# Row-packed 64-row products fed by full transposes, pairs first, and a second layer one group behind

## The chip, the cores and the metric

The kernel runs on one core of a Trainium2 chip. The metric is device time in microseconds: the median of three timed runs, and beside it one profiled execution with its trace.

## The reference

An mLSTM cell runs over four batches of eight heads (768 steps, 40 values a head). Its output, 3072 rows of 320 values, goes through a mixture of eight experts, of which each row uses the one with the largest logit.

```python
# cell, for each step t: C, n are decayed and added to, then read with q
h_tilde = np.einsum('bhde,bhe->bhd', C, qt)
denom = np.maximum(np.abs(nq), 1.0)
y[:, :, t] = o * h_tilde / denom
# experts; x has 3072 rows of D = 320, w1 is (8, 320, 1024), w2 is (8, 1024, 320)
logits = x @ w_gate
expert_idx = np.argmax(logits, axis=1)
...
for e in range(E):
    h = np.maximum(x_sorted[lo:hi] @ w1[e], 0.0)
    y_sorted[lo:hi] = h @ w2[e]
return gate_w[:, None] * y_sorted[inv_perm]
```

## The kernel before

The cell is done in 24 blocks of 128 steps. Rows are then scattered to DRAM by expert and read back in tiles of 128 rows. An expert gets three tiles in any case: a group of two, which is read early, and a group of one. Five more tiles are for what overflows, and for those the weights of the expert concerned are copied within SBUF (`wx`). Two groups of two (experts 0 and 1) run while the cell ends; the other six groups of two, eight groups of one and the five overflow tiles run in the main loop below.

The 320 values of a row are 128 + 128 + 64. The 64 last are done as pairs: w1's last 64 rows are held twice, on partitions 0 to 63 for the first half of the hidden columns and on 64 to 127 for the second half, so that two 64-row matmuls can run side by side. For that the last 64 columns of a tile are transposed onto both partition halves.

```python
    def weights_in(e, n=1):                                   # w1, cast to bf16 on the way
        nc.gpsimd.dma_start(
            w1_all[:, e, : FL * F].rearrange("p (a f) -> p a f", f=F),
            moe_w1[e, : FL * 128, :].rearrange("(a p) f -> p a f", p=128),
        )
        for i in range(2):
            nc.gpsimd.dma_start(
                w1_all[64 * i : 64 * i + 64, e, FL * F :], moe_w1[e, FL * 128 :, i * HF * 128 : (i + 1) * HF * 128],
            )

    def weights_out(e0, n):                                   # w2
        e = slice(e0, e0 + n)
        nc.gpsimd.dma_start(
            w2_all[:, e].rearrange("p e a d -> p (e a) d"), moe_w2[e].rearrange("e (a p) d -> p (e a) d", p=128),
        )
...
    def turn(g):
        n = g["n"]
        src = g["xg"] if "xg" in g else xg[g["e"]][g["k"]]
        g["xT"] = spot("xT", [128, DB, n * 128], BF16)
        tp = spot("tp", [128, DB, n * 128], BF16)
        for j in range(n):
            for db in range(DB):
                at = src[:, j, db * 128 : min(Dm, (db + 1) * 128)]
                if db < FL:
                    nc.tensor.transpose(tp[:, db, j * 128 : (j + 1) * 128], at, ident_b[:])
                    continue
                for r in range(2):
                    nc.tensor.transpose(tp[64 * r : 64 * r + 64, db, j * 128 : (j + 1) * 128], at, ident_b[:])
        nc.vector.tensor_copy(g["xT"], tp)

    def layer1(g, u):
        n = g["n"]
        per = 4 // n
        w, xT = g["w"][0], g["xT"]
        v = u // 2 * per
        if u == 0:
            g["h"] = spot("h", [128, FB, n * 128], BF16)
        if u % 2 == 0:
            g["hp"] = [spot("hp", [128, per, n * 128], F32) for _ in range(2)]
            for i in range(per):
                for a in range(2):
                    c = FL * F + (v + i) * 128
                    r = slice(64 * a, 64 * a + 64)
                    nc.tensor.matmul(
                        g["hp"][a][:, i, :], lhsT=w[r, c : c + 128], rhs=xT[r, FL, :], start=(i == 0), stop=False,
                        skip_group_check=True,
                    )
        a = u % 2
        hp = g["hp"][a]
        for i in range(per):
            for db in range(FL):
                c = db * F + (a * HF + v + i) * 128
                nc.tensor.matmul(
                    hp[:, i, :], lhsT=w[:, c : c + 128], rhs=xT[:, db, :], start=False, stop=(db == FL - 1),
                    skip_group_check=True,
                )
        dst = g["h"][:, a * HF + v : a * HF + v + per, :]
        if a == 0:
            nc.vector.tensor_relu(dst, hp)
        else:
            nc.scalar.activation(dst, hp, AF.Relu)

    def layer2(g, j):
        zp = spot(g.get("zp", "zp"), [128, Dm], F32)
        for fb in range(FB):
            nc.tensor.matmul(
                zp, lhsT=g["h"][:, fb, j * 128 : (j + 1) * 128], rhs=g["w"][1][:, fb, :],
                start=(fb == 0), stop=(fb == FB - 1),
            )
        zo = spot("zo", [128, Dm], F32)
        nc.scalar.copy(zo, zp)
        at = g["to"] if "to" in g else s_idx[:, g["e"], g["si"] + j : g["si"] + j + 1]
        ins = nc.gpsimd.indirect_dma_start(
            out=out[:, :], out_offset=bass.IndirectOffsetOnAxis(ap=at, axis=0),
            in_=zo, in_offset=None, bounds_check=N - 1, oob_is_err=False,
        )
        if g.get("apart", True):
            apart(ins, "rows_out")
        if j + 1 < g["n"]:
            pause()

    def pause():
        nc.gpsimd.memset(rest[:], 0.0)

```

`zp` of the two early groups is taken from the same four PSUM buffers as `hp`. The main loop has four `hp`, two `zp` and two `tp` buffers, three each of `h` and `xT`, and sixteen of `zo`. In it the order is fixed as written:

```python
    order = [(2, 0), (3, 0), (0, 1), (1, 1), (4, 0), (2, 1), (5, 0), (3, 1), (4, 1), (6, 0), (5, 1), (7, 0), (6, 1), (7, 1)]
    groups = [...] + [dict(n=1, x=x) for x in range(XU)]      # (expert, part): part 0 has two tiles, part 1 has one
    ...
    pieces = extras()
    ready(groups[0])
    for i, g in enumerate(groups):
        nw = g.get("e", E) + 3
        x = i - len(order) + XW
        if 0 <= x < XU:
            groups[len(order) + x]["w"] = fetch(expert_of(x))
        if g.get("k") == 0 and nw < E:
            weights_in(nw, 1)
            weights_out(nw, 1)
        for u in range(FB * g["n"] // 4):
            layer1(g, u)
        if i + 1 < len(groups):
            ready(groups[i + 1])
        if 1 <= i < 5:
            next(pieces, None)
        if i == 5:
            for e_ in range(E):
                blank(e_)
            for x in range(XU):
                collect(groups[len(order) + x], row_of(x), invx[:, x : x + 1])
        for j in range(g["n"]):
            layer2(g, j)
```

`ready` computes the target rows and does `turn`, the transposes. `fetch` copies an overflow tile's weights. `warm(n)` issues n matmuls of 512 columns whose result isn't used; `warm(3)` stands at the last block of the cell and `warm(2)` after the first early transposes.

Of the kernel before, what the change touches and what calls it, by code (L numbers as in the profile page):

```python
# [8 lines left out]
F32 = mybir.dt.float32  # L9
BF16 = mybir.dt.bfloat16  # L10
# [9 lines left out]
def kernel(  # L20
# [13 lines left out]
    nc = tc.nc  # L34
    B, H, S, D = q.shape
    BH = B * H
    NB = S // 128
    N = B * S
    Dm = H * D
    E = moe_w_gate.shape[1]  # L40
    F = moe_w1.shape[2]
    FB = F // 128
    NT = N // 128
    PR = H // 2
    DP = 64
# [5 lines left out]
    dch = []  # L51
    d0 = 0
# [5 lines left out]
    FL = DB - 1  # L58
    HF = FB // 2
    wch = [d0 if dsz == 128 else Dm - 128 for d0, dsz in dch]  # L60
    assert NT * 128 == N and FB * 128 == F and D <= DP and dch[FL][1] == 64


    NJ = 3
# [110 lines left out]
    xg = [(x_all[:, NE * e : NE * (e + 1), :], x_all[:, NE * E + e : NE * E + e + 1, :]) for e in range(E)]  # L175

    def weights_in(e, n=1):
        nc.gpsimd.dma_start(
            w1_all[:, e, : FL * F].rearrange("p (a f) -> p a f", f=F),
            moe_w1[e, : FL * 128, :].rearrange("(a p) f -> p a f", p=128),  # L180
        )
        for i in range(2):
            nc.gpsimd.dma_start(
                w1_all[64 * i : 64 * i + 64, e, FL * F :], moe_w1[e, FL * 128 :, i * HF * 128 : (i + 1) * HF * 128],
            )

    def weights_out(e0, n):
        e = slice(e0, e0 + n)
        nc.gpsimd.dma_start(
            w2_all[:, e].rearrange("p e a d -> p (e a) d"), moe_w2[e].rearrange("e (a p) d -> p (e a) d", p=128),  # L190
        )

    def apart(ins, group):
# [24 lines left out]
    def spot(kind, shape, dtype):  # L218
        i = turns[kind] = turns.get(kind, -1) + 1
        at = spots[kind][i % len(spots[kind])]  # L220
        if isinstance(at, tuple):
            tag, pool = at
            return pool.tile(shape, dtype, name=kind, tag=tag)[:]
        n = 1
        for m in shape[1:]:
            n *= m
        at = at[:, :n]
        return at.rearrange("p (a b) -> p a b", b=shape[2]) if len(shape) == 3 else at

    def turn(g):  # L230
        n = g["n"]
        src = g["xg"] if "xg" in g else xg[g["e"]][g["k"]]
        g["xT"] = spot("xT", [128, DB, n * 128], BF16)
        tp = spot("tp", [128, DB, n * 128], BF16)
        for j in range(n):
            for db in range(DB):
                at = src[:, j, db * 128 : min(Dm, (db + 1) * 128)]
                if db < FL:
                    nc.tensor.transpose(tp[:, db, j * 128 : (j + 1) * 128], at, ident_b[:])
                    continue  # L240
                for r in range(2):
                    nc.tensor.transpose(tp[64 * r : 64 * r + 64, db, j * 128 : (j + 1) * 128], at, ident_b[:])
        nc.vector.tensor_copy(g["xT"], tp)

    def layer1(g, u):
        n = g["n"]
        per = 4 // n
        w, xT = g["w"][0], g["xT"]
        v = u // 2 * per
        if u == 0:  # L250
            g["h"] = spot("h", [128, FB, n * 128], BF16)
        if u % 2 == 0:
            g["hp"] = [spot("hp", [128, per, n * 128], F32) for _ in range(2)]
            for i in range(per):
                for a in range(2):
                    c = FL * F + (v + i) * 128
                    r = slice(64 * a, 64 * a + 64)
                    nc.tensor.matmul(
                        g["hp"][a][:, i, :], lhsT=w[r, c : c + 128], rhs=xT[r, FL, :], start=(i == 0), stop=False,
                        skip_group_check=True,  # L260
                    )
        a = u % 2
        hp = g["hp"][a]
        for i in range(per):
            for db in range(FL):
                c = db * F + (a * HF + v + i) * 128
                nc.tensor.matmul(  # L267
                    hp[:, i, :], lhsT=w[:, c : c + 128], rhs=xT[:, db, :], start=False, stop=(db == FL - 1),
                    skip_group_check=True,
                )  # L270
        dst = g["h"][:, a * HF + v : a * HF + v + per, :]
# [23 lines that stand above are left out]
# [12 lines left out]
    with tc.tile_pool(name="ring", bufs=1) as ring_pool, \  # L307
# [256 lines left out]
        def warm(n):  # L564
            j = ps1.tile([128, 512], F32, name="junk", tag="tk")
            for _ in range(n):
                nc.tensor.matmul(
                    j[:], lhsT=ident_b[:], rhs=st[NT - 1]["dA"][:].rearrange("p j t -> p (j t)"), start=True, stop=True,
                )
# [37 lines left out]
        for s in range(-3, NT):  # L607
            P, odd = (s - 4) // 2, s % 2
            last = s == NT - 1
            do(scores, s + 1)  # L610
            do(transposes, s + 2)
            if s == -3:
                masks()
            if s == -2:
                gates()
                router()
            do(values, s + 2)
            if odd and s > E and sent <= (s - 5 if s > 2 * PE_ + 4 else s - 6):
                send(sent)
                sent += 1  # L620
            if s == NT - 5:
                weights_in(0, 1)
            pair = not odd and 0 <= P
            if pair:
                gate(P)
            do(states, s)
            do(load, s + 6 if s >= -1 else -1)
            if pair:
                rank(P, s - 1)
            if last:  # L630
                warm(3)
            do(xtrans, s - 1)
            do(ogate, s + 2)
            do(attend, s)
            if pair:
                place(P)
                if P == PE_:
                    even_out(s - 1)
            if s == 2 * PE_ + 4:
                keep_rows(s - 4)  # L640
                keep_rows(s - 3)
            elif s != 2 * PE_ + 5:
                do(keep_rows, s - 4)
            do(rows, s)
            if odd and 0 <= (s - 3) // 2:
                logits((s - 3) // 2, s - 1)
                choose((s - 3) // 2)
                count((s - 3) // 2)
            upto = s - 4 if s >= 2 * PE_ + 4 else s - 5
            if s > E and sent <= upto:  # L650
                send(sent)
                sent += 1
            if 0 <= s < E:
                clear(s)
            late_consts(s + 1)
            if s == 2 * PE_ + 5:
                for e in range(E):
                    receive(e, 0)
            if s == NT - 4:
                weights_out(0, 1)  # L660
            if s == NT - 3:
                weights_in(1, 1)
            if s == NT - 2:
                weights_out(1, 1)
# [12 lines left out]
        first, second = early  # L677
        targets(0, 0)
        turn(first)
        warm(2)  # L680
        xtrans(NT - 1)
        layer1(first, 0)
        logits(P0 + 1, NT)
# [131 lines left out]
# [16 lines that stand above are left out]
                blank(e_)  # L831
            for x in range(XU):
                collect(groups[len(order) + x], row_of(x), invx[:, x : x + 1])
        for j in range(g["n"]):
            layer2(g, j)
    one_order.close()
    nx = nc.values_load(xe[0:1, NX : NX + 1], min_val=0, max_val=NX)
    with tc.If(nx > XU):
# [40 lines left out]
```

## Time and profile before

| | before |
|---|---|
| time, median of three runs | 217.75 us (216.98 to 218.1) |
| span of the profiled run | 217.2 us |
| mean granted TensorE clock | 0.984 |
| TensorE matmul busy | 192.3 us (89%) in 2048 matmuls |
| TensorE weight loads busy | 151.8 us (70%) |
| VectorE, ScalarE, GpSimd busy | 57%, 54%, 64% |
| moved by DMA | 44.32 MB, mean 204 GB/s |
| chain that ended last | TensorE 46%, GpSimd 20%, "issue" 14%, VectorE 9%, DMA 5% |

PE is TensorE's matmuls, PEld its weight loads, DVE VectorE, ACT ScalarE, POOL GpSimd, SP the queue of the sync engine. Matmuls overlap in the array, so the time from one start to the next counts, not the length of one. A line such as L267 is a line of the kernel printed above; an arrow (out<-in) names what is written and read; "[0.44 <-DMA x]" says that the engine sat idle for 0.44 us until x. The chain that ended last is followed back from the last instruction, at each step to what released it. "issue" is idle time that nothing in the profile explains.

### The profile page before, as it was taken

What the parts mean: (1) busy time and instruction counts of PE and PEld (TensorE: products, weight loads), DVE (VectorE), ACT (ScalarE), POOL (GpSimd) and SP (SyncE); (2) the same over time, 40 slices, a digit from 0 to 9 for tenths busy, and PEclk for the clock granted to TensorE, in tenths of its full rate; (3) what the DMA queues carried; (4) which work ended last, traced back from release to release, by engine and by line L of the source; (5) the groups of instructions that cost most, each with busy time, mean ns of one, the idle gap of its engine ahead of it and who ended that gap; (6) DMA issues with size and microseconds to landing.
All of it is one profiled execution on the core that took longest, in us unless ns stands there. A gap on an engine that the chain in (4) does not pass through costs nothing.

```text
span 217.2 us, 5727 instructions
## 1 busy us (share of the span) xinstructions
PE 192.3 (89%) x2048; PEld 151.8 (70%) x2057; DVE 124.8 (57%) x410; ACT 117.3 (54%) x273; POOL 139.3 (64%) x238
## 2 busy tenths in 40 slices
PE   1299999999999999979899998969999986999970
PEld 1168788899998899978786755647667654676740
DVE  7746667677787878797776342345833332333320
ACT  2458657797789897896751552323333322332330
POOL 6036786644869889749999489838656786253221
PEclk9999999999999999999998899999999999999996
DMA  7999999989999989994799999999999999985310
GB/s 139 197 198 190 205 205 204 231 156 254 178 193 173 195 161 206 193 204 84 142 184 262 222 205 150 193 254 233 216 229 245 231 290 408 409 317 201 149 46 10
DMA packets 120782, 44.32 MB, mean 204 GB/s; under 512 B 102506, under 2 KB 115821, under 8 KB 120752
## 3 DMA queue, kind: packets, MB, share of 16 engines
q1 hardware_dynamic: 105456, 25.34, 55.9%
q0 software_dynamic: 14832, 18.38, 40.3%
q8 instruction: 17, 0.28, 0.5%
q10 hardware_dynamic: 464, 0.21, 0.4%
q14 instruction: 13, 0.11, 0.2%
HBM read 39.30 MB, written 9.37 MB: 224 GB/s over the span
## 4 chain that ended last, share of the span: by engine, by line
PE 46%; POOL 20%; issue 14%; DVE 9%; DMA 5%; ACT 3%; POOLq 1%; ACTq 0%; DVEq 0%
POOL out_dram L287 7%; PE hp L474 6%; PE zp L280 5%; DMA w_all<-in_moe_w_dram 5%; PE hp L406 5%; PE tk L368 4%; POOL x_sorted L579 4%; PE dC L414 4%; PE hp L267 4%; PE tq L368 3%; PE xt L451 3%; PE sA L386 3%; PE sA L381 2%; POOL x_sb L444 2%; POOL rest L297 2%
## 5 line engine op out<-in xcount | busy, mean ns | idle before, releaser
L273 DVE TENSOR_SCALAR h<-hp 128x512 bf16<-128x512 f32 x25 | 17.3, 692 | 40.6 <-PE hp L267 26.3
L287 POOL DMA_INDIRECT out_dram<-zo,s_idx x20 | 20.0, 1002 | 16.3 <-ACT zo L285 10.0
L275 ACT ACTIVATE h<-hp 128x512 bf16<-128x512 f32 x25 | 14.9, 597 | 25.2 <-PE hp L267 19.9
L579 POOL DMA_INDIRECT x_sorted<-x_all,slots x24 | 25.3, 1054 | 4.9 <-issue 3.9
L444 POOL TENSOR_TENSOR x_sb<-x_sb,den 128x320 f32<-128x320 f32 x23 | 16.8, 729 | 17.2 <-DVE den L442 17.1
L280 PE MATMUL zp<-w_all,h 128*128 128x320 bf16 x160 | 24.5, 300 | 3.5 <-DMA w_all<-in_moe_w_dram 1.6
L280 PEld LDWEIGHTS <-h 128*128 128x128 bf16 x200 | 17.7, 98 | 13.2 <-DVE h L273 2.7
L285 ACT COPY zo<-zp 128x320 f32<-128x320 f32 x25 | 10.7, 426 | 27.2 <-PE zp L280 23.7
L267 PEld LDWEIGHTS <-w_all 128*128 128x128 bf16 x256 | 18.4, 98 | 5.6 <-issue 3.4
L393 ACT CAST dB<-sB 128x512 bf16<-128x512 f32 x24 | 14.0, 585 | 13.7 <-PE sB L387 11.5
L267 PE MATMUL hp<-xT,w_all 128*128 128x128 bf16 (+1 forms) x224 | 21.1, 243 | 0.0
L406 PE MATMUL hp<-C_sb,qT 104*128 104x82 f32 x160 | 20.7, 272 | 0.0
L368 PE MATMUL tk<-ident,kq 128*104 128x128 f32 x96 | 16.4, 296 | 4.2 <-DMA kq<-in_k_dram 4.2
L406 PEld LDWEIGHTS hp<-C_sb,qT 104*128 104x128 f32 x160 | 19.4, 192 | 0.3
L453 ACT COPY xT<-xt 128x384 f32<-128x384 f32 x24 | 11.6, 482 | 13.5 <-PE xt L451 12.5
L356 POOL CAST vAb<-vA 128x328 bf16<-128x328 f32 x24 | 11.0, 459 | 11.7 <-DVE vA L354 11.7
L474 PE MATMUL hp<-wg_sb,xT 128*128 128x8 f32 x144 | 18.0, 258 | 0.0
L414 PE MATMUL dC<-vA,kq 128*104 128x82 f32 x160 | 17.9, 254 | 0.0
L394 POOL TENSOR_SCALAR_AFFINE_SELECT dB<-dB 128x512 bf16<-128x512 bf16 x24 | 16.5, 689 | 1.7 <-ACT dB L393 1.5
L474 PEld LDWEIGHTS hp<-wg_sb,xT 128*128 128x128 f32 x144 | 17.4, 195 | 0.1
L391 DVE TENSOR_TENSOR dA<-sA,cmask 128x512 bf16<-128x512 f32 x24 | 16.0, 669 | 1.4 <-PE sB L387 1.4
L414 PEld LDWEIGHTS dC<-vA,kq 128*104 128x104 f32 x160 | 16.3, 172 | 0.0
(160 smaller groups left out, 455.8 us busy)
## 6 DMA issues: line engine op xcount, KB each, us to landing
wx<-w_all SPq DMA_DIRECT2D x10, 640.0 KB
w_all<-in_moe_w_dram POOLq DMA_DIRECT2D x8, 640.0 KB
w_all<-in_moe_w_dram POOLq DMA_DIRECT2D x8, 512.0 KB
kq<-in_k_dram SPq DMA_DIRECT2D x24, 160.0 KB
kq<-in_q_dram SPq DMA_DIRECT2D x24, 160.0 KB
v<-in_v_dram SPq DMA_DIRECT2D x24, 160.0 KB
o_sb<-in_o_gate_dram SPq DMA_DIRECT2D x24, 160.0 KB
x_sorted<-zrow POOLq DMA_DIRECT2D x8, 241.5 KB
```

Of the source, the lines that this page charges most:

```text
L267: nc.tensor.matmul(hp[:, i, :], lhsT=w[:, c : c + 128], rhs=xT[:, db, :], start=False, stop=(db == FL - 1), skip_group_check=True,)
L273: nc.vector.tensor_relu(dst, hp)
L280: nc.tensor.matmul(zp, lhsT=g["h"][:, fb, j * 128 : (j + 1) * 128], rhs=g["w"][1][:, fb, :], start=(fb == 0), stop=(fb == FB - 1),)
L287: ins = nc.gpsimd.indirect_dma_start(out=out[:, :], out_offset=bass.IndirectOffsetOnAxis(ap=at, axis=0), in_=zo, in_offset=None, bounds_ch ...
L368: nc.tensor.transpose(tp[:, j, :], two(d[n], j), ident[:])
L391: nc.vector.tensor_tensor(d["dA"][:], sA[:], cmask[:, None, :].to_broadcast([128, PR, 128]), op=ALU.mult)
L394: nc.gpsimd.affine_select(d["dB"][:], d["dB"][:], compare_op=ALU.is_ge, fill=0.0, base=0, pattern=[[0, PR], [1, 128]], channel_multiplier=-1,)
L406: nc.tensor.matmul(hp[:, 2 * j * D1 : (2 * j + 2) * D1], lhsT=d["qT"][:, j, :], rhs=st["C"][:, j].rearrange("p h d -> p (h d)"), start=(j ...
L414: nc.tensor.matmul(st["dC"][:, j], lhsT=two(d["k"], j), rhs=d["vA"][:, 2 * j : 2 * j + 2, :], start=(c == 0 and j == 0), stop=True, skip_g ...
L444: eng.tensor_tensor(x3d, x3d, den[:].unsqueeze(2).to_broadcast([128, H, D]), op=ALU.mult)
L474: nc.tensor.matmul(lg[:, i * E : (i + 1) * E], lhsT=st[t]["xT"][:, db * 128 : (db + 1) * 128], rhs=wg_sb[:, db, :], start=(fresh and i == ...
L579: ins = nc.gpsimd.indirect_dma_start(out=xs[:, :], out_offset=bass.IndirectOffsetOnAxis(ap=slots[:, t : t + 1], axis=0), in_=x_all[:, t, : ...
```

## The change

Four things are altered in the expert stage. First, each tile is transposed four times in full, from columns 0, 192, 128 and 64 on, 128 columns each; the third has the columns 128 to 191 on partitions 0 to 63 and the fourth has them on 64 to 127, so these two feed the 64-row pairs, and the first two the full matmuls. The pairs thus use w1's rows 128 to 191. The aim is that transposes and the matmuls around them use the array in the same way. Second, all pairs of a group are issued first, into all product buffers of the group, where a two-tile group did half of them before each half of its full matmuls. Third, in the main loop a group's second layer is issued after the next group's first layer, so that its relu need not be waited for. Fourth, w2 is loaded so that a partition gets two neighbouring rows in one run of 2560 bytes instead of two runs of 1280; hidden unit 256a + 2p + j then sits on partition p, and w1's columns are read with a step of two to match. Besides, `warm` has two more matmuls in one place and one more in the other.

```diff
--- before.py
+++ after.py
@@ -58,7 +58,9 @@
     FL = DB - 1
     HF = FB // 2
     wch = [d0 if dsz == 128 else Dm - 128 for d0, dsz in dch]
-    assert NT * 128 == N and FB * 128 == F and D <= DP and dch[FL][1] == 64
+    assert NT * 128 == N and FB * 128 == F and D <= DP and Dm == 5 * 64
+    parts = [0, 192, 128, 64]
+    NP = len(parts)
 
 
     NJ = 3
@@ -175,19 +177,22 @@
     xg = [(x_all[:, NE * e : NE * (e + 1), :], x_all[:, NE * E + e : NE * E + e + 1, :]) for e in range(E)]
 
     def weights_in(e, n=1):
+        at = moe_w1.offset + e * Dm * F
         nc.gpsimd.dma_start(
             w1_all[:, e, : FL * F].rearrange("p (a f) -> p a f", f=F),
-            moe_w1[e, : FL * 128, :].rearrange("(a p) f -> p a f", p=128),
+            bass.AP(moe_w1.tensor, at, [[F, 128], [parts[1] * F, 2], [1, F]]),
         )
         for i in range(2):
             nc.gpsimd.dma_start(
-                w1_all[64 * i : 64 * i + 64, e, FL * F :], moe_w1[e, FL * 128 :, i * HF * 128 : (i + 1) * HF * 128],
+                w1_all[64 * i : 64 * i + 64, e, FL * F :],
+                moe_w1[e, parts[2] : parts[2] + 64, i * HF * 128 : (i + 1) * HF * 128],
             )
 
     def weights_out(e0, n):
         e = slice(e0, e0 + n)
         nc.gpsimd.dma_start(
-            w2_all[:, e].rearrange("p e a d -> p (e a) d"), moe_w2[e].rearrange("e (a p) d -> p (e a) d", p=128),
+            w2_all[:, e].rearrange("p e (a j) d -> p (e a) (j d)", j=2),
+            moe_w2[e].rearrange("e (a p j) d -> p (e a) (j d)", p=128, j=2),
         )
 
     def apart(ins, group):
@@ -230,17 +235,15 @@
     def turn(g):
         n = g["n"]
         src = g["xg"] if "xg" in g else xg[g["e"]][g["k"]]
-        g["xT"] = spot("xT", [128, DB, n * 128], BF16)
-        tp = spot("tp", [128, DB, n * 128], BF16)
+        g["xT"] = spot("xT", [128, NP, n * 128], BF16)
+        tp = spot("tp", [128, NP, n * 128], BF16)
         for j in range(n):
-            for db in range(DB):
-                at = src[:, j, db * 128 : min(Dm, (db + 1) * 128)]
-                if db < FL:
-                    nc.tensor.transpose(tp[:, db, j * 128 : (j + 1) * 128], at, ident_b[:])
-                    continue
-                for r in range(2):
-                    nc.tensor.transpose(tp[64 * r : 64 * r + 64, db, j * 128 : (j + 1) * 128], at, ident_b[:])
+            for a, d0 in enumerate(parts):
+                nc.tensor.transpose(tp[:, a, j * 128 : (j + 1) * 128], src[:, j, d0 : d0 + 128], ident_b[:])
         nc.vector.tensor_copy(g["xT"], tp)
+
+    def column(fb):
+        return fb // 2 * 256 + fb % 2
 
     def layer1(g, u):
         n = g["n"]
@@ -249,23 +252,22 @@
         v = u // 2 * per
         if u == 0:
             g["h"] = spot("h", [128, FB, n * 128], BF16)
-        if u % 2 == 0:
-            g["hp"] = [spot("hp", [128, per, n * 128], F32) for _ in range(2)]
-            for i in range(per):
+            g["hp"] = [spot("hp", [128, per, n * 128], F32) for _ in range(2 * n)]
+            for k in range(HF):
                 for a in range(2):
-                    c = FL * F + (v + i) * 128
+                    c = FL * F + column(k)
                     r = slice(64 * a, 64 * a + 64)
                     nc.tensor.matmul(
-                        g["hp"][a][:, i, :], lhsT=w[r, c : c + 128], rhs=xT[r, FL, :], start=(i == 0), stop=False,
-                        skip_group_check=True,
+                        g["hp"][k // per * 2 + a][:, k % per, :], lhsT=w[r, c : c + 255 : 2], rhs=xT[r, FL + a, :],
+                        start=(k % per == 0), stop=False, skip_group_check=True,
                     )
         a = u % 2
-        hp = g["hp"][a]
+        hp = g["hp"][u]
         for i in range(per):
             for db in range(FL):
-                c = db * F + (a * HF + v + i) * 128
+                c = db * F + column(a * HF + v + i)
                 nc.tensor.matmul(
-                    hp[:, i, :], lhsT=w[:, c : c + 128], rhs=xT[:, db, :], start=False, stop=(db == FL - 1),
+                    hp[:, i, :], lhsT=w[:, c : c + 255 : 2], rhs=xT[:, db, :], start=False, stop=(db == FL - 1),
                     skip_group_check=True,
                 )
         dst = g["h"][:, a * HF + v : a * HF + v + per, :]
@@ -628,7 +630,7 @@
             if pair:
                 rank(P, s - 1)
             if last:
-                warm(3)
+                warm(5)
             do(xtrans, s - 1)
             do(ogate, s + 2)
             do(attend, s)
@@ -677,7 +679,7 @@
         first, second = early
         targets(0, 0)
         turn(first)
-        warm(2)
+        warm(3)
         xtrans(NT - 1)
         layer1(first, 0)
         logits(P0 + 1, NT)
@@ -831,8 +833,10 @@
                 blank(e_)
             for x in range(XU):
                 collect(groups[len(order) + x], row_of(x), invx[:, x : x + 1])
-        for j in range(g["n"]):
-            layer2(g, j)
+        if i:
+            for j in range(groups[i - 1]["n"]):
+                layer2(groups[i - 1], j)
+    layer2(groups[-1], 0)
     one_order.close()
     nx = nc.values_load(xe[0:1, NX : NX + 1], min_val=0, max_val=NX)
     with tc.If(nx > XU):
```

## The prediction

> **What bounds the kernel now.** I read the chain that ended last first, because the engines' shares average two stages (the recurrent cells up to about 117 us, the experts after it).
>
> ```profile
> 133.01 11.71 DMA w_all<-in_moe_w_dram
> 144.86 2.33 PE zp L280 x16
> 147.52 0.57 PE hp L267 x8
> 148.12 0.70 DVE h L273
> 148.86 1.26 PE zp L280 x8
> ```
>
> Columns: start, length, what. Up to 133 us POOL's scatters and weight issues lead, then one weight transfer, and from 144.86 us the chain is TensorE with a relu (L273) between two of its steps. (After about 170 us it lists POOL scatters and "issue", but POOL is only following: each scatter waits for the copy after the second layer.) So the expert stage is priced from TensorE's own timeline. Two groups of it, one of two tiles (from 153.26) and one of one tile (from 196.04); start, length, line, shape, count:
>
> ```profile
> 153.26 0.39 PE L258 MATMUL hp<-xT,w_all 64*128 64x256 bf16 x4
> 153.59 1.05 PE L267 MATMUL hp<-xT,w_all 128*128 128x256 bf16 x8
> 154.57 0.39 PE L258 MATMUL hp<-xT,w_all 64*128 64x256 bf16 x4
> 154.89 1.05 PE L267 MATMUL hp<-xT,w_all 128*128 128x256 bf16 x8
> 155.77 0.28 PE L239 MATMUL tp<-ident_b,x_all 128*128 128x128 bf16 x2
> 155.98 0.25 PE L242 MATMUL tp<-ident_b,x_all 128*64 128x128 bf16 x2
> 156.16 2.35 PE L280 MATMUL zp<-w_all,h 128*128 128x320 bf16 x16
> ...
> 196.04 0.40 PE L258 MATMUL hp<-xT,wx 64*128 64x128 bf16 x8
> 196.37 1.07 PE L267 MATMUL hp<-xT,wx 128*128 128x128 bf16 x16
> 197.28 0.28 PE L239 MATMUL tp<-ident_b,xgx 128*128 128x128 bf16 x2
> 197.48 0.25 PE L242 MATMUL tp<-ident_b,xgx 128*64 128x128 bf16 x2
> 197.84 1.26 PE L280 MATMUL zp<-wx,h 128*128 128x320 bf16 x8
> 199.03 0.40 PE L258 MATMUL hp<-xT,wx 64*128 64x128 bf16 x8
> ```
>
> Only starts count, as lengths overlap. 16 plain 128-column matmuls take 197.28 - 196.37 = 0.91 us, 57 ns each; 256 columns take about 109 ns (0.88 for the last eight of the two-tile group). By that pace eight need 0.87, but the first block lasts 0.98: 0.11 more, where the 64-row form follows. Four 64-row matmuls, two at a time, need 2 x 0.109 = 0.22 but take 0.33: again 0.11 more. Four transposes of a tile should need 4 x 0.057 = 0.23 and take 156.16 - 155.77 = 0.39. In the one-tile group there are 0.56 us from 197.28 to 197.84, so 0.17 of it waits for the relu. Two more views matter. The timeline of POOL, with a wait before an instruction in brackets:
>
> ```profile
> 138.90 0.53 POOL L183 DMA_DIRECT2D w_all<-in_moe_w_dram  x1 [0.44 <-DMA w_all<-in_moe_w_dram]
> ...
> 148.66 0.53 POOL L183 DMA_DIRECT2D w_all<-in_moe_w_dram  x1 [0.76 <-DMA w_all<-in_moe_w_dram]
> ...
> 156.37 0.53 POOL L183 DMA_DIRECT2D w_all<-in_moe_w_dram  x1 [0.76 <-DMA w_all<-in_moe_w_dram]
> ```
>
> [...] That dates landings: expert 3's first-layer block at 138.9, expert 4's at 148.6, expert 5's at 156.3. And the busy times by microsecond (engines, then PEclk, the third last column):
>
> ```profile
> 118.00:119.00 1.00, 1.00 (x4) 0.62 (x5) 0.90 (x7) 0.00 (x0) 1.00 (x2) 0.54 1.12 243
> 119.00:120.00 1.00, 0.99 (x7) 0.31 (x5) 0.46 (x1) 0.46 (x2) 1.00 (x2) 0.50 1.07 237
> 120.00:121.00 1.00, 1.00 (x8) 0.77 (x6) 0.00 (x0) 0.59 (x5) 0.01 (x1) 0.50 1.20 242
> ```
>
> The clock is halved for about 3.4 us from 118.1.
>
> [...] The trace shows only contiguous bf16 weights; with 41-column products (line 426) load and matmul follow each other every 25 ns, while fp32 ones (line 406: eight in 0.85 us) take 106 ns. No run here shows a step of two. [...] TensorE was not idle before 118 us, only broken up by gaps (0.37 us before 115.23). [...]
>
> **The change part by part.**
>
> Transposes: 4 full ones instead of 2 full and 2 half ones. All have the shape of the matmuls around them, so two mode changes go: 0.39 to 0.23, 0.16 to 0.17 us per tile, for 29 tiles (2 x 2 early, 12 in the six two-tile groups, 13 single). The copy of the transposed tile grows: 357 ns for 384 and 557 ns for 768 columns give 0.52 ns per column, so 424 and 690 ns. VectorE is idle most of this stage and the copy will lie under the second layer of the group before.
>
> Pairs first: in a two-tile group the pairs of both halves come together, so two of four mode changes go: 2.51 becomes 2.30 us, in 8 groups. One-tile groups had all pairs first already.
>
> Second layer one group behind: the relu waits after the transposes go. I count 0.11 + 0.18 + 0.25 + 0.17 + 4 x 0.17 + 0.57 = 2.0 us (0.57 for the last group, which has no transposes to hide it).
>
> Weights in runs of 2560 bytes: [...] It is off the path except for the first experts. For it w1 is read with a column step of two. If loads only became twice as slow, 50 ns still hide under 57 ns.
>
> Warm: three more idle matmuls of 0.22 us in the turn of the stages, mostly in gaps; if they keep the clock up, up to a microsecond is won before 125 us. I count zero to -0.5.
>
> The sum can't simply be added, because weights pin the start. In the new order the first main group's first layer (from about 134.5) is followed by the second group's at 134.5 + 2.30 + 0.46 = 137.3, as its own second layer is put off. That one reads expert 3's w1, which lands at 138.9. So TensorE waits there about 1.6 us, in place of the 1.64 us before 144.86. From 138.9 on: five two-tile groups 5 x (2.30 + 2.28) = 22.9; thirteen single ones 13 x (1.23 + 1.19) = 31.5; 21 tiles of transposes x 0.23 = 4.8; the second layer put off from the first group 2.3. Total 61.5, so TensorE ends at 200.4 against 211.05. The old trace has one more loss in that stretch, gaps put down to "issue" and slow steps between 175.98 and 184.81, together 3.3 us over what the same groups cost elsewhere (1.1 and 2.2), while the copies of weights for the last tiles run at 400 GB/s and ACT and VectorE stand still too. I expect about half of it again: 202. With the unchanged tail of 6.2 us (last copy, scatter, end) the span is 208.2, and the timed runs lie 0.5 above the profiled span: 208.7. I add 0.5 for a weight that comes late and take off part of the clock's gain: 209.
>
> **The rivals.**
>
> [...] Then a load takes the 106 ns of line 406 instead of hiding: 24 loads x 50 ns = 1.2 us in each of 13 single groups, +16 us in all, hidden at 256 columns; about 225 us. For it: nothing in this trace has such a step. [...]
>
> Transfers become the bound. From 117 to 191 us the DMA engines are full (share 1.1 to 1.3), so a TensorE that is ten microseconds faster might only wait. For it: the 11.7 us for one weight pair. Against: in the old run experts 5 to 7 land 3 to 10 us ahead of need, and with the new order expert 6's issue no longer stands behind the first main group's scatters. The needs in my schedule (expert 4's w1 at 150.3 against 148.6, expert 5's at 158 against 156.3) leave 1.7 us. If each pinned a group I would see 212 to 214.
>
> PSUM takes back the pairs. All four product buffers are wanted at a group's start. In the second early group two of them hold second-layer sums just being copied (0.43 us), so 0.4 us is lost there; later, a second layer of 1.19 us or more lies between, longer than a relu. Worth +0.4, up to +2 if I am wrong: 211.
>
> **Range and chances.** 206 if the copy stage does not stall and the clock stays up; 213 if weights pin two or three groups. Slower needs the slow weight loads. Faster by over 2% (below 213.4) 0.84, within 2% 0.09, slower 0.07.
>
> **What would show it.** Right: transposes of a tile in 0.23 us with no gap to the next matmul; one-tile groups every 2.65 us instead of 2.99; one wait for weights near 137 to 139 us and none at a first product of the second layer; fast clock near 118 to 122. Wrong: first-layer matmuls at 128 columns spaced near 107 ns; waits for weights at several groups between 150 and 180; or the copy stage standing still for longer than 3 us.

## The result, and the profile after

The changed kernel takes 211.31 us (median of four runs, 210.68 to 212.62) against 217.64 us for the kernel before. The ratio is 0.972, with a 95% interval from 0.967 to 0.977, so it is faster, by 6.3 us where 8.7 was forecast. The span of the profiled run is 208.9 us against 217.2. Runs that lie more than 1.5% above the fastest of the same kernel are left out of all ratios and medians, and traces that come from such runs (the base and the copy left out in the second set of experiments, the two tries, the idle matmuls) are read for the order of issue and its waits only.

TensorE's own timeline of the changed kernel, for the same kinds of group as in the prediction (start, length, line, shape, count; L260 are the pairs, L269 the full products, L242 the transposes, L282 the second layer):

```profile
158.46 0.61 PE L260 MATMUL hp<-xT,w_all 64*128 64x256 bf16 x8
159.01 1.92 PE L269 MATMUL hp<-xT,w_all 128*128 128x256 bf16 x16
160.76 0.39 PE L242 MATMUL tp<-ident_b,x_all 128*128 128x128 bf16 x4
160.99 1.25 PE L282 MATMUL zp<-w_all,h 128*128 128x320 bf16 x8
...
186.50 0.40 PE L260 MATMUL hp<-xT,wx 64*128 64x128 bf16 x8
186.83 1.07 PE L269 MATMUL hp<-xT,wx 128*128 128x128 bf16 x16
187.73 0.39 PE L242 MATMUL tp<-ident_b,xgx 128*128 128x128 bf16 x4
187.96 1.25 PE L282 MATMUL zp<-w_all,h 128*128 128x320 bf16 x8
189.14 0.40 PE L260 MATMUL hp<-xT,wx 64*128 64x128 bf16 x8
```

A two-tile first layer now takes 160.76 - 158.46 = 2.30 us (2.51 before). Four transposes take 0.23 (0.39), and the second layer follows with no gap. A one-tile group comes every 2.64 us (2.99). Its eight 64-row matmuls take 186.83 - 186.50 = 0.33 us, 41 ns each, where a full one takes 56. The 16 products of L269 take 0.90 us (0.91 before), so the column step of two in the weights costs nothing here.

Two waits of TensorE for transfers are left in the main loop; in brackets the idle time before the line and what ended it:

```profile
138.86 0.97 PE L260 MATMUL hp<-xT,w_all 64*128 64x256 bf16 x8 [1.31 <-DMA w_all<-in_moe_w_dram]
139.77 1.92 PE L269 MATMUL hp<-xT,w_all 128*128 128x256 bf16 x16
...
199.09 0.40 PE L260 MATMUL hp<-xT,wx 64*128 64x128 bf16 x8 [1.86 <-DMA wx<-w_all]
...
200.33 2.34 PE L282 MATMUL zp<-wx,h 128*128 128x320 bf16 x16
```

The first is the wait on expert 3's weights that the prediction put there. The pairs behind it take 139.77 - 138.86 = 0.91 us, where two-tile groups without a wait need 0.55, since their weight loads wait for that transfer as well (0.27 us before the one at 139.22). The second wait the prediction did not have: the last overflow tile waits for the copy of its weights. The gaps of 3.3 us that the old trace has near 176 to 184 us are absent. The chain that ended last, by engine, shows the same shift, from POOL and "issue" to TensorE:

```profile
PE 64%; POOL 9%; DVE 8%; issue 8%; ACT 6%; DMA 3%; POOLq 0%; ACTq 0%; DVEq 0%
```

The clock near 118 us, where it was halved before (the third last column is PEclk), is full:

```profile
118.00:119.00 1.00, 1.00 (x11) 0.65 (x7) 0.86 (x7) 0.00 (x0) 1.00 (x2) 1.00 1.12 243
119.00:120.00 1.00, 0.20 (x2) 0.09 (x1) 0.97 (x4) 0.76 (x4) 1.00 (x2) 1.00 1.10 244
```

In the second line TensorE is busy for only 0.20 us: it waits 0.90 us for the wider copy of the first early tiles' transposes (L243), which VectorE starts at 119.37 us and does in 0.68 us (118.91 and 0.55 before). It cost nothing that shows: expert 3's weights, on which the main loop waits, are issued at 131.10 us, against 131.19 before.

### The profile page after: what moved, and what is told of

It is laid out like the page before. It is cut to its first block, busy times and chain, and to the rows that moved or that the text cites. A ratio compares the mean times of both kernels' runs of the same rounds, so it can differ in the third digit from the quotient of the medians.

```text
span 208.9 us, 5733 instructions
## 1 busy us (share of the span) xinstructions
PE 184.8 (88%) x2051; PEld 153.3 (73%) x2060; DVE 125.7 (60%) x410; ACT 117.0 (56%) x273; POOL 137.7 (66%) x238
## 4 chain that ended last, share of the span: by engine, by line
PE 64%; POOL 9%; DVE 8%; issue 8%; ACT 6%; DMA 3%; POOLq 0%; ACTq 0%; DVEq 0%
PE zp L282 10%; PE hp L269 9%; PE hp L408 7%; PE hp L476 6%; PE tk L370 5%; PE dC L416 5%; PE tq L370 4%; PE xt L453 3%; PE sA L383 3%; PE sA L388 3%; DMA w_all<-in_moe_w_dram 3%; PE hp L260 3%; POOL out_dram L289 3%; POOL x_sorted L581 2%; PE tp L242 2%
## 5 line engine op out<-in xcount | busy, mean ns | idle before, releaser
L282 PE MATMUL zp<-w_all,h 128*128 128x320 bf16 x160 | 24.0, 299 | 0.0
L282 PEld LDWEIGHTS <-h 128*128 128x128 bf16 x200 | 18.8, 98 | 6.2
L269 PEld LDWEIGHTS <-w_all 128*128 128x128 bf16 x256 | 19.0, 98 | 3.8 <-issue 1.1
L269 PE MATMUL hp<-xT,w_all 128*128 128x128 bf16 (+1 forms) x224 | 20.1, 243 | 0.0
```

The source lines that it names most:

```text
L269: nc.tensor.matmul(hp[:, i, :], lhsT=w[:, c : c + 255 : 2], rhs=xT[:, db, :], start=False, stop=(db == FL - 1), skip_group_check=True,)
L282: nc.tensor.matmul(zp, lhsT=g["h"][:, fb, j * 128 : (j + 1) * 128], rhs=g["w"][1][:, fb, :], start=(fb == 0), stop=(fb == FB - 1),)
```

## The experiments

My theory after reading the trace was: TensorE's work shrank as forecast, but the end is pinned by the weight transfers and the five weight copies behind them, so that anything won or lost in TensorE's order counts only beyond the 1.9 us wait at the end. The rival was that the parts add up and the wait is one more item in the sum. Each ratio below is to the kernel before, run beside it. The runs were made in three sets: the four that undo a part; the base, the added buffer, the copy left out and the first try with earlier weights; the base, the copy left out, the second try and the idle matmuls. In the last two sets the intervals are wide. The first set has no base of its own. The changed kernel's own ratio was 0.972 beside the prediction and 0.984 in the third set, so a difference of 0.012 between two sets is not an effect by itself, and for the first set the traces have to carry the reading.

**The half transposes back.**

```diff
-    NP = len(parts)
+    NP = 3
...
-            for a, d0 in enumerate(parts):
+            for a, d0 in enumerate(parts[:2]):
                 nc.tensor.transpose(tp[:, a, j * 128 : (j + 1) * 128], src[:, j, d0 : d0 + 128], ident_b[:])
+            for r in range(2):
+                nc.tensor.transpose(
+                    tp[64 * r : 64 * r + 64, 2, j * 128 : (j + 1) * 128], src[:, j, 128:192], ident_b[:]
+                )
...
-    ... rhs=xT[r, FL + a, :],
+    ... rhs=xT[r, FL, :],
```

> The changed kernel with the half transposes back (two full and two 64-column ones per tile), everything else as changed. Theory A (the end is pinned by the copy of the last overflow tile's weights, for which the changed kernel's TensorE waits 1.86 us at 197.2 us): a tile's transposes take 0.39 us again instead of 0.22, 21 tiles x 0.165 = 3.5 us after 138.9 us, but the 1.86 us wait is eaten up first, so about +1.6 us on the changed kernel, and no wait for a weight copy left in the trace. Theory B (the parts simply add up): +3.5 us, the wait of 1.9 us still there.

Ratio 0.981 (0.976 to 0.986), against 0.972 for the changed kernel, which was measured apart from this set: the difference is 0.009, about 1.9 us, with intervals that just overlap (0.976 and 0.977). TensorE's timeline near the end:

```profile
200.06 0.40 PE L264 MATMUL hp<-xT,wx 64*128 64x128 bf16 x8
200.39 1.07 PE L273 MATMUL hp<-xT,wx 128*128 128x128 bf16 x16
201.30 2.34 PE L286 MATMUL zp<-wx,h 128*128 128x320 bf16 x16
```

There is no wait before the last overflow tile at 200.06. From the end of the wait for expert 3's weights to the last second layer it is 201.30 - 138.44 = 62.9 us, against 200.33 - 138.86 = 61.5 in the changed kernel: 1.4 us. That is what theory A expects (1.6) and not the 3.5 us of extra transposes.

**The pairs of a two-tile group in two halves again.** The first `if` is the one the kernel before has:

```diff
-            g["hp"] = [spot("hp", [128, per, n * 128], F32) for _ in range(2 * n)]
-            for k in range(HF):
+        if u % 2 == 0:
+            g["hp"] = [spot("hp", [128, per, n * 128], F32) for _ in range(2)]
+            for i in range(per):
                 for a in range(2):
...
-        hp = g["hp"][u]
+        hp = g["hp"][a]
```

> The changed kernel with the pairs of a two-tile group again in two halves. Five such groups after 138.9 us x 0.21 = 1.05 us of mode changes. Theory A (end pinned by the last weight copy): no difference (0 to +0.3 us), the last wait 1.0 us shorter. Theory B (parts add): +1.0 to +1.4 us.

Ratio 0.977 (0.974 to 0.981); the interval overlaps that of the changed kernel. The last wait is shorter by 0.67 us, and the last second layer starts 200.58 - 139.08 = 61.5 us after expert 3's weights, as in the changed kernel:

```profile
139.08 0.68 PE L261 MATMUL hp<-xT,w_all 64*128 64x256 bf16 x4 [1.58 <-DMA w_all<-in_moe_w_dram]
...
199.34 0.40 PE L261 MATMUL hp<-xT,wx 64*128 64x128 bf16 x8 [1.19 <-DMA wx<-w_all]
200.58 2.34 PE L283 MATMUL zp<-wx,h 128*128 128x320 bf16 x16
```

In that run, then, the work the pairs save is taken back by the wait at the end. The two ratios lie 1.2 us apart, which would suit theory B, but with intervals that overlap they decide nothing; the reading for theory A rests on the trace alone.

**The second layer straight after its own first layer.**

```diff
-        if i:
-            for j in range(groups[i - 1]["n"]):
-                layer2(groups[i - 1], j)
-    layer2(groups[-1], 0)
+        for j in range(g["n"]):
+            layer2(g, j)
```

> The changed kernel with the second layer straight after its own group's first layer and the next transposes, as before. Relu waits of about 2.0 us come back, the wait for expert 3's first-layer weights near 138 us goes and one for its second-layer weights near 143 us comes, about 0.5 us longer. Theory A (end pinned by the last weight copy): +0.6 us, the wait at the last overflow tile gone. Theory B (parts add): +2.5 us.

Ratio 0.984 (0.979 to 0.989), about 2.6 us more than the changed kernel by the two ratios. The traces agree: expert 3's weights are issued alike (131.05 and 131.10 us) and TensorE ends 2.3 us later, at 203.72 + 1.26 = 204.98 against 200.33 + 2.34 = 202.67. The last wait is gone, as theory A says, but the time is what theory B says. That is chance, as B keeps the last wait; both had the price of the relu wait wrong. The second layers of three one-tile groups in TensorE's timeline, and the last:

```profile
188.77 1.26 PE L282 MATMUL zp<-w_all,h 128*128 128x320 bf16 x8 [0.17 <-DVE si L782]
...
191.20 0.39 PE L242 MATMUL tp<-ident_b,xgx 128*128 128x128 bf16 x4
191.76 1.26 PE L282 MATMUL zp<-wx,h 128*128 128x320 bf16 x8 [0.17 <-DVE si L782]
...
194.75 1.26 PE L282 MATMUL zp<-wx,h 128*128 128x320 bf16 x8 [0.18 <-DVE si L782]
...
203.72 1.26 PE L282 MATMUL zp<-wx,h 128*128 128x320 bf16 x8 [0.40 <-DVE h L275]
```

The groups come every 2.99 us, which is exactly the step of the kernel before, although its transposes are the short ones. From the start of the transposes to the second layer it is 0.56 us in both. The relu holds the second layer for that long in both; shorter transposes only uncover more of it, 0.33 instead of 0.17 us. So in one-tile groups the full transposes are worth nothing without the later second layer, and the two together are worth the 0.35 us a group that the changed kernel shows. The first wait is longer too: 2.20 us for expert 3's second-layer weights, at 144.50, in place of 1.31.

**Runs of 1280 bytes, column step one.**

```diff
-            w2_all[:, e].rearrange("p e (a j) d -> p (e a) (j d)", j=2),
-            moe_w2[e].rearrange("e (a p j) d -> p (e a) (j d)", p=128, j=2),
+            w2_all[:, e].rearrange("p e a d -> p (e a) d"), moe_w2[e].rearrange("e (a p) d -> p (e a) d", p=128),
...
-        return fb // 2 * 256 + fb % 2
+        return fb * 128
...                                        # and c : c + 128 for c : c + 255 : 2 in both products
```

> The changed kernel with w2 loaded in runs of 1280 bytes and w1 read with a column step of one. If the longer runs speed the weights up [...] time +0 to +0.5 us. If the step of two slows the weight loads anywhere: first-layer matmuls at 128 columns closer than 57 ns and a faster kernel, -0.5 us or more. If neither matters: same, and the spacing stays 56 to 57 ns.

Ratio 0.984 (0.979 to 0.988), about 2.5 us more than the changed kernel by the two ratios: far more than I gave it. The queue that issues the copies shows when the weights are in, since the first half of the first copy waits for expert 7's first-layer weights and the second half for its second-layer weights (3.8 us in three waits and 2.7 us in one, in the changed kernel). First the changed kernel, then this one:

```profile
174.32 0.59 SPq L790 DMA_DIRECT2D wx<-w_all  x1
177.80 0.49 SPq L791 DMA_DIRECT2D wx<-w_all  x1
```

```profile
175.58 0.59 SPq L789 DMA_DIRECT2D wx<-w_all  x1
179.23 0.49 SPq L790 DMA_DIRECT2D wx<-w_all  x1
```

With 1280-byte runs they are in 1.3 and 1.4 us later. The other three kernels of this set, with long runs, have these issues at 173.9 to 174.4 and 177.1 to 178.7, so the first delay is clear of their spread and the second by only 0.5 us. Nor is it an even delay for each expert: TensorE's wait for expert 3's first-layer weights ends at 138.90 here and at 138.86 in the changed kernel. But nothing of it is hidden. TensorE's timeline has two waits for copies in place of one:

```profile
195.25 0.40 PE L259 MATMUL hp<-xT,wx 64*128 64x128 bf16 x8 [0.83 <-DMA wx<-w_all]
...
200.57 0.61 PE L259 MATMUL hp<-xT,wx 64*128 64x128 bf16 x8 [2.60 <-DMA wx<-w_all]
201.10 1.89 PE L268 MATMUL hp<-xT,wx 128*128 128x128 bf16 x16
202.79 2.69 PE L281 MATMUL zp<-wx,h 128*128 128x320 bf16 x16
```

Together 3.43 us against 1.86, and after the long one the 16 products take 1.69 us (from 201.10 to 202.79) instead of 0.90. The clock is what slowed them: it is halved there (the third last column), while behind the wait in the changed kernel it stays full (1.00 from 199 to 203 us).

```profile
201.00:202.00 1.00, 1.00 (x13) 0.90 (x10) 0.00 (x0) 0.00 (x0) 0.00 (x0) 0.50 0.49 190
202.00:203.00 1.00, 1.00 (x11) 0.94 (x9) 0.69 (x1) 0.00 (x0) 0.00 (x0) 0.50 0.04 15
```

With the pairs (0.53 instead of 0.34) and the second layer (2.69 instead of 2.34) the half clock costs some 1.3 us. TensorE ends at 205.48, 2.8 us after the changed kernel's 202.67; so 1.6 of that is longer waiting and most of the rest the clock. Elsewhere 16 products at 128 columns take 0.91 us with a step of one and 0.90 with two.

**The base again, and one more buffer.** The changed kernel was run once more:

> The changed kernel itself on this chip, as the base for the runs beside it. 210.5 to 212 us; a wait of 1 to 2.5 us for the last overflow tile's weight copy, and no gaps put down to issue while the copies run (if those gaps of the old kernel come from the copies as such, they should turn up here in some form).

It gave no ratio that can be used, and its trace is not as expected: while the copies ran, TensorE stood still for 6.18 us, and the last tile did not wait for its copy.

```profile
186.38 0.61 PE L260 MATMUL hp<-xT,w_all 64*128 64x128 bf16 x8 [6.18 <-DVE xT L243]
```

Beside it, five buffers for the weight copies (`XW = 5` for `XW = 4`):

> The changed kernel with five instead of four buffers for the overflow tiles' weight copies, so that the fifth copy need not wait for the first overflow tile to be done. Theory A (the DMA queue is what is late: the copies follow each other without a break): the fifth copy is issued some 2 us earlier but lands when it did, the wait stays 1.5 to 2 us, time the same within 0.5 us. Theory B (the buffer is what is late): the wait goes, -1.5 to -1.9 us.

Ratio 0.985 (0.978 to 0.992), which without a base beside it says little. The copies are more telling. First the fourth and fifth of the changed kernel, then of this one:

```profile
186.01 0.48 SPq L790 DMA_DIRECT2D wx<-w_all  x1
186.63 1.75 SPq L791 DMA_DIRECT2D wx<-w_all  x1
189.78 0.49 SPq L790 DMA_DIRECT2D wx<-w_all  x1
191.88 0.49 SPq L791 DMA_DIRECT2D wx<-w_all  x1
```

```profile
187.57 0.49 SPq L790 DMA_DIRECT2D wx<-w_all  x1
188.19 1.31 SPq L791 DMA_DIRECT2D wx<-w_all  x1
190.80 0.48 SPq L790 DMA_DIRECT2D wx<-w_all  x1
191.42 1.35 SPq L791 DMA_DIRECT2D wx<-w_all  x1
```

With a buffer to spare the fifth copy still starts 3.2 us after the fourth, where it was 3.8 us. A copy moves two times 640 KB, so 1.31 MB in about 3.3 us, some 400 GB/s, which is also what the slices of the changed kernel's page show there (399, 391, 382). The buffer did hold back the second half of the fifth copy, at 191.88 (1.4 us, put down to the second layer that reads the buffer), but TensorE waits for the first half, which carries w1. For that half the buffer is not what is late; the queue is. My expectation of an issue 2 us earlier was wrong in that the issue, too, still comes 3.2 us after the one before it. The wait at the end can't be compared in this run, because TensorE itself stood still for 2.24 us while the copies began:

```profile
176.52 2.34 PE L282 MATMUL zp<-w_all,h 128*128 128x320 bf16 x16
181.09 0.61 PE L260 MATMUL hp<-xT,w_all 64*128 64x256 bf16 x8 [2.24 <-issue]
```

**One copy less.** The last overflow tile takes the weights of the tile before it. This leaves a fifth of the copies out, and up to 128 rows of the output are then not the reference's.

```diff
-            groups[len(order) + x]["w"] = fetch(expert_of(x))
+            groups[len(order) + x]["w"] = fetch(expert_of(x)) if x < XW else groups[len(order) + x - 1]["w"]
```

> The changed kernel without the fifth weight copy: the last overflow tile is multiplied with the weights of the tile before it, so up to 128 rows of the output are not the reference's. Both theories on the queue and on the buffer: the wait before the last overflow tile goes, -1.9 us. If the time does not fall by more than 0.5 us, the end is pinned by something else, such as the scatters.

Ratio 0.987 (0.982 to 0.992), again without a base. So it was run once more, with the changed kernel beside it:

> The changed kernel as the base for the runs beside it, on a chip that is hoped to be less disturbed. 210.5 to 212 us, a wait of 1 to 2.5 us for the last overflow tile's weight copy unless the engines stand still while the copies run, in which case that wait is hidden behind the stand-still.

> As a_copy4, once more beside its base: the last overflow tile uses the weights of the tile before it, so up to 128 rows of the output are not the reference's, and one of five weight copies is left out. If the copies pin the end: no wait before the last overflow tile and 1.5 to 2 us less than after_2. If the wait only hides another limit: within 0.5 us of after_2.

The base has a ratio of 0.984 (0.976 to 0.992) in that set and the kernel without the fifth copy 0.979 (0.970 to 0.988). The medians are 214.3 and 212.8 us, 1.5 us apart, but the intervals overlap widely. The base's TensorE timeline (first) repeats the wait at the end, and the other one has none before its last tile (199.43), with 0.50 us left before the fourth:

```profile
200.95 0.40 PE L260 MATMUL hp<-xT,wx 64*128 64x128 bf16 x8 [1.87 <-DMA wx<-w_all]
201.28 1.82 PE L269 MATMUL hp<-xT,wx 128*128 128x128 bf16 x16
202.89 3.28 PE L282 MATMUL zp<-wx,h 128*128 128x320 bf16 x16
```

```profile
196.78 0.40 PE L260 MATMUL hp<-xT,wx 64*128 64x128 bf16 x8 [0.50 <-DMA wx<-w_all]
...
199.43 0.40 PE L260 MATMUL hp<-xT,wx 64*128 64x128 bf16 x8
...
200.66 2.34 PE L282 MATMUL zp<-wx,h 128*128 128x320 bf16 x16
```

That the wait comes from the amount to be copied is shown by the trace; its price of 1.5 us in the timed runs is likely, not proven. In the base's trace the wait again costs more than its length: the clock is halved behind it (0.50 from 202 to 204 us), the 16 products take 202.89 - 201.28 = 1.61 us instead of 0.90 and the second layer 3.28 instead of 2.34. TensorE ends there at 206.17 us and at 203.00 without the fifth copy. How often the clock drops behind this wait is not known: in the first trace of the same kernel it did not.

**Expert 3's weights earlier, first try.** `weights_in(3, 1)` and `weights_out(3, 1)` stand ahead of the last two scatters of rows.

> A version that may beat both: expert 3's weights are issued ahead of the last two scatters of rows instead of behind them, at about 127.3 instead of 131.1 us, where the DMA engines run dry from about 131.5 to 134.5 us. Theory A (the weight stream, then the copies, pin the end): first-layer weights land near 135.5 us, the wait of 1.3 us at 137.4 goes, all later landings and the copies come 2 to 3 us earlier, -1.5 to -3 us. Rival: the last rows reach DRAM 3 to 4 us later, the one-tile groups' rows come late and TensorE waits for them near 140 us instead; no gain or +1 us.

Ratio 1.000 (0.991 to 1.008): all of the gain is lost. The wait of the rival came. The weights came in time (the pairs at 138.58 no longer wait for them), but the last scatter was issued at 134.37 us instead of 129.66, and the rows of the one-tile groups came late:

```profile
138.58 0.61 PE L260 MATMUL hp<-xT,w_all 64*128 64x256 bf16 x8 [0.78 <-DVE xT L243]
...
145.57 0.61 PE L242 MATMUL tp<-ident_b,x_all 128*128 128x128 bf16 x4 [4.52 <-DMA x_all<-x_sorted]
```

How much of the loss is this wait is not shown: the same trace has a stand-still of 3.59 us at 182.12, as the base of its set has one, and that base gives no ratio to compare with.

**Second try: no idle fills between the scatters.** The four `pause()` after the early `send(t)` are left out.

> A version that may beat both: the four idle fills of 0.55 us behind the scatters of the last rows are left out on POOL, so that expert 3's weights are issued at about 128.9 instead of 131.1 us and no row is sent later. If the weight stream and the copies behind it pin the end: expert 3's first-layer weights land near 136.7 instead of 138.7, the wait of 1.3 us at 137.4 goes, the copies start and end up to 2 us earlier, 1.3 to 2 us less than after_2. Rival: the transfers are limited by their bytes from 117 us on, the earlier issue only queues longer, within 0.5 us of after_2.

Ratio 0.972 (0.964 to 0.980) beside the base's 0.984 (0.976 to 0.992); runs at 211.5, 211.9 and 213.1 us against 214.25 to 215.6. The medians differ by 2.4 us, the intervals overlap a little. In the trace the weights are issued at 131.27 us where the base has 132.98, and TensorE no longer waits for expert 3's first-layer weights. But the trace doesn't show the gain that was argued: the copies start no earlier (176.83 against the base's 176.50), and TensorE waits for them longer, 4.0 us in two waits against 1.87:

```profile
197.36 0.40 PE L260 MATMUL hp<-xT,wx 64*128 64x128 bf16 x8 [1.24 <-DMA wx<-w_all]
...
202.84 0.40 PE L260 MATMUL hp<-xT,wx 64*128 64x128 bf16 x8 [2.77 <-DMA wx<-w_all]
```

That is the rival, an earlier issue that only queues longer. The ratio is the lowest of its set, but that this kernel beats the changed one is not shown.

**The idle matmuls as before.** `warm(3)` and `warm(2)`.

> The changed kernel with the idle matmuls as before (three and two). If they hold the clock up: the half clock comes back for about 3.4 us near 118 us. If the clock there matters to the time: +0.5 to +1 us. If only POOL's chain of scatters counts there: expert 3's weights are issued at 131 us as ever, within 0.3 us of after_2.

Ratio 0.979 (0.971 to 0.987); runs from 211.9 to 214.9 us around a median of 213.9, against 214.3 for the base. No effect of the idle matmuls can be told apart from noise. What they do to the clock near 118 us stays open.

## Why the prediction was right, and where its terms were off

**The mode changes, the relu, the pairs: right.** A mode change is here what the trace before shows where a 64-row or 64-column form meets the full one: about 0.1 us lost, as in the 0.98 us for eight products that need 0.87 by their pace. What loses it was not shown. Transposes 0.23 us (forecast 0.23), a two-tile first layer 2.30 (2.30), a one-tile group 2.64 (2.65), no gap between transposes and second layer. In the second early group the pairs take 0.89 us from 127.98 to 128.87 where they take 0.55 in groups without a wait. The last of their weight loads start at 128.56, just as ScalarE's copy of a second-layer sum out of one of those buffers ends (128.09 + 0.42), so 0.34 us goes to the product buffers, forecast 0.4.

**The wait on expert 3's weights: right.** They were expected at 138.9 and came at 138.86; the wait is 1.31 us, with the 0.36 us lost in the pairs behind it 1.67, against 1.6.

**The step of two: right.** 0.90 us for 16 products (0.91 with a step of one). The first rival, in which a load with a step of two takes the 106 ns of line 406, was the author's estimate and didn't occur.

**"Off the path except for the first experts": the step that failed.** The longer runs were given a small gain for each expert, the author's estimate, which no run had shown; 1.3 to 1.4 us was measured by the last. And the sum treated transfers as hidden after 138.9, having compared landings with needs only for experts 4 to 7. The copies for the overflow tiles wait for the last of those landings and run one behind the other, and the fifth was never held against its need at 197 us. It is 1.86 us late, so the transfers of the second rival did pin the end, only at the last tile and not between 150 and 180 us. By the experiments the longer runs are worth about 2.5 us (forecast: next to nothing); in the traces it is 2.8 us, of which 1.6 is waiting and the rest mostly the halved clock behind it. In the traces the transposes are worth less than their TensorE time (1.4 of 3.5 us), and the pairs nothing that can be seen.

**The stand-still: wrong by half, the other way.** I kept half of the old 3.3 us. None came back in the changed kernel's trace, which gave 1.65 us and nearly cancelled the unforeseen wait of 1.86. So it is partly luck that TensorE ended at 202.67 us, forecast 202, and that the span was 208.9, forecast 208.2.

**The step from span to time: mis-sized.** I added 0.5 us. In both profiled runs the time is 1.8 us above its own span (210.68 and 208.9; 218.99 and 217.2). The old kernel's profiled run lay 1.3 us above that kernel's median of 217.64, in a trace with a 3.3 us stand-still, and the changed kernel's 0.6 us below its median. So a gain of 8.3 us between the two traces is 6.3 us between the medians.

**The clock: full as hoped, nothing in the time.** The half clock went (1.00 at 118 us, 0.54 before), though no run shows that the idle matmuls did it; that they might was the author's estimate. But the weights of expert 3 are issued when they were before (131.10 and 131.19 us), as POOL's scatters set that: the last starts at 129.66 (129.74 before).

## What to carry to other kernels

A saving on the busiest engine was worth here only what the latest transfer left of it (1.4 us in the traces for 3.5 us of transposes), so hold every transfer up to the last one against its need in the new schedule, not only those near the change. Two savings around one wait did not simply add up: shorter transposes alone only showed more of the relu's delay (2.99 us for a one-tile group, as before), and the reordering alone left the mode changes (2.81), but together they took 0.35 us off it (2.64). An early weight issue that pushed back a scatter on the same queue brought a longer wait than the one it took away (4.52 us for 1.31).

## What the runs showed of the hardware that I had not expected

Sixteen matmuls with weights at a column step of two run at the same 56 to 57 ns each as with contiguous ones. The clock dropped behind some short waits of TensorE: it was halved (0.50) behind 2.60 us with the short runs and behind 1.87 us in the changed kernel's third trace, and stayed full (1.00) behind 1.86 us in its first. Engines stood still together for some microseconds while copies within SBUF ran at about 400 GB/s (391 to 424 from 178 to 186 us in the kernel before). There ScalarE's copy at 182.65 us came 2.7 us late, with "remote" given as what it waited for, in the same stretch in which TensorE lost 3.3 us:

```profile
182.65 0.43 ACT L285 COPY zo<-zp 128x320 f32<-128x320 f32 x1 [2.70 <-remote]
```

The variant with five buffers stood still for 2.24 us there, and the changed kernel itself, in the same set, for 6.18. All four traces of that set have such gaps (the longest of each 2.05 to 6.18 us), and those of the first and the third set and the one beside the prediction have none. So it doesn't go with the kernel; what causes it stays open, and no run was made for it.
